# Part B of a decode kernel: keys loaded in whole rows, half of them copied aside by GpSimd, and a softmax in two halves

## The chip, the cores and the metric

The kernel runs on one core of one Trainium2 chip. The time is device microseconds of one execution, as the median of the runs shown. A core has five engines that run beside each other and wait for each other by semaphores: TensorE (PE in the profile), VectorE (DVE), ScalarE (ACT), GpSimd (POOL) and SyncE (SP). Sixteen DMA engines move data between the chip's memory (HBM) and the on-chip memory (SBUF).

## The reference

Two attention steps for one new token (decode) with a cache, side by side. Part A has 32 query heads on 8 key heads and looks at the last W = 2048 positions; part B has 32 query heads with a key head each and looks at all 8192.

```python
def _B_ref(x, k_cache, v_cache, wq, wo):     # x 4x1x512, caches 4x32x8192x128, bf16
    q = (x @ wq).reshape(B, Sq, H, Dh).transpose(0, 2, 1, 3)
    scores = einsum("bhqd,bhkd->bhqk", q, k_cache) * (Dh ** -0.5)
    p = softmax(scores, axis=-1)
    o = einsum("bhqk,bhkd->bhqd", p, v_cache)
    return o.transpose(0, 2, 1, 3).reshape(B, Sq, H * Dh) @ wo
# _A_ref: the same on k_cache[:, :, Sk - W:], v_cache[:, :, Sk - W:] of 8 heads, each repeated 4 times
return concatenate([a, b], axis=-1)
```

Part B's two caches are 2 x 268 MB of the 587 MB that the kernel reads.

## The kernel before, in words

All instructions are first written into one list for each engine (`sch.add`, with what each waits for, and `sch.add_dma` for transfers), and these lists are then issued in order. Where windows between marks repeat (`whole_B`), TensorE, VectorE and ScalarE run them as a loop; SyncE and GpSimd run straight-line code. So the order on an engine is the order in which the Python code adds its instructions, and an instruction that waits holds up everything behind it on its engine.

The work comes in chunks: 8 of part A (numbers 0 to 7), then 32 of part B (8 to 39, `NCA` = 8, `NC` = 40). A chunk of part B is four heads of one batch entry: 256 tiles of 128x128 keys and as many of values, 64 KB in each of 128 partitions, 8.39 MB each. The SBUF tensor `kv` has ten slots of 16 KB per partition: part B's keys lie in slots 0 to 3, its values in 4 to 7, and slots 8 and 9, keys of part A, hold `wol` in part B.

For one chunk (`whole_B`, line 802), with eight tiles to a group and 32 groups:

- `emit_T` transposes eight key tiles on TensorE into one of three PSUM banks `tr`; VectorE (two of three groups, L491) or ScalarE (every third, L489) copies the bank to one of four buffers `kt`. Two groups later (`SLAG`) `emit_S` multiplies it with the query `qq` into the scores `sc`, which have two banks, one for each half of the chunk.
- `stats_rowmax` takes the maxima of each half on VectorE (L560). After the last scores, `stats_gmax` and `stats_bc` make one maximum per head over all rows and its negative `negb` (a transpose and a broadcast on TensorE, two small VectorE steps), and `exp_B` writes the probabilities `pbb` on ScalarE in eight instructions (L606). TensorE meanwhile reorders four blocks of rows of the output weight `wos` (`reorder`), which VectorE copies to `wol` (`take_wol`, L722), and runs fillers (`keep_busy`).
- `emit_pv` multiplies 256 value tiles with the probabilities into the bank `po`; `norm_sum` sums the probabilities over partitions and inverts the sum; `norm_out` writes the weighted output `oz`. The output projection of a chunk (`emit_fin`) runs in the next chunk, after its second group of transposes, and adds up in the PSUM bank `fin` to the end.

The transfers are issued on SyncE in the order wos (every fourth chunk), keys, values (`dma_B`, line 365). Keys come in two halves of 32 KB rows, and the two halves of the buffer come free after the 16th and the 32nd group's transposes. Values come in one transfer of 64 KB rows that waits for the previous chunk's last value product; the last chunks, and the second chunk's values, come in smaller pieces. GpSimd waits for each landing and passes it on to TensorE as a count of groups (`relay`, semaphores `r_k` and `r_v`), so that TensorE's loop can wait on one count. The last two pieces of part A's output weight are loaded at the very end.

## Time and profile before

| | before |
|---|---|
| median of 3 runs | 1370.96 us (1370.92 to 1371.13) |
| the profiled execution, its own time | 1370.91 us |
| its span, first to last instruction | 1369.2 us |
| mean granted TensorE clock | 0.981 |
| VectorE, ScalarE, GpSimd busy | 744.0, 514.2, 9.8 us |
| key and value transfers of part B | 69 and 42 |

The profile is of one execution. A group row reads: line, engine, operation, output <- inputs, shapes, count | busy us, mean ns of one | idle time of the engine ahead of them and what ended it. A timeline row reads: start, length, engine, line, operation and how many of them in a row [idle time before, what ended it]. A row of the chain of waits reads: start, length, what the end was waiting for; the start of a DMA row is its issue and its end the landing. A DMA line counts packets (one to a partition row, and small ones that report the end) and their bytes.

### The profile page before, as it was taken

What the parts mean: (1) busy time and instruction counts of PE and PEld (TensorE: products, weight loads), DVE (VectorE), ACT (ScalarE), POOL (GpSimd) and SP (SyncE); (2) the same over time, 40 slices, a digit from 0 to 9 for tenths busy, and PEclk for the clock granted to TensorE, in tenths of its full rate; (3) what the DMA queues carried; (4) which work ended last, traced back from release to release, by engine and by line L of the source; (5) the groups of instructions that cost most, each with busy time, mean ns of one, the idle gap of its engine ahead of it and who ended that gap; (6) DMA issues with size and microseconds to landing.
All of it is one profiled execution on the core that took longest, in us unless ns stands there. A gap on an engine that the chain in (4) does not pass through costs nothing.

```text
span 1369.2 us, 61524 instructions
## 1 busy us (share of the span) xinstructions
PE 1246.1 (91%) x27801; PEld 1111.7 (81%) x27801; DVE 744.0 (54%) x1335; ACT 514.2 (38%) x649; POOL 9.8 (1%) x29
## 2 busy tenths in 40 slices
...
DMA  9999999999999999999999999999999999999998
GB/s 398 425 428 438 423 432 435 429 434 438 431 431 438 422 433 435 433 439 429 433 433 426 430 437 432 433 438 429 433 431 429 433 436 433 436 433 428 424 426 362
DMA packets 20948, 587.52 MB, mean 429 GB/s; under 512 B 2344, under 2 KB 2368, under 8 KB 4416
## 3 DMA queue, kind: packets, MB, share of 16 engines
...
q8 instruction: 15, 0.25, 0.1%
...
q10 hardware_dynamic: 32, 0.01, 0.0%
HBM read 587.21 MB, written 0.01 MB: 429 GB/s over the span
## 4 chain that ended last, share of the span: by engine, by line
DMA 59%; PE 37%; DVE 2%; issue 1%; ACT 1%; SPq 0%; POOLq 0%; ACTq 0%; DVEq 0%
DMA kv<-in_B_k_cache_dram 36%; PE tr L424 18%; DMA kv<-in_B_v_cache_dram 16%; PE po L426 9%; PE sc L426 8%; DMA wor<-in_A_wo_dram 3%; DMA kv<-in_A_k_cache_dram 2%; DMA kv<-in_B_wq_dram 2%; PE fin L426 1%; PE tr L426 1%; PE ms L426 1%; ACT pba L628 0%; DVE kt L491 0%; DVE sA L544 0%; DVE kv L722 0%
## 5 line engine op out<-in xcount | busy, mean ns | idle before, releaser
L424 PE MATMUL tr<-identb,kv 128*128 128x128 bf16 x8704 | 667.6, 221 | 48.4 <-POOLq L74 40.7
L491 DVE COPY kt<-tr 128x1024 bf16<-128x1024 bf16 x736 | 502.0, 691 | 261.3 <-PE tr L424 258.5
L489 ACT ACTIVATE kt<-tr 128x1024 bf16<-128x1024 bf16 x352 | 359.7, 1024 | 700.8 <-PE tr L424 700.7
L424 PEld LDWEIGHTS tr<-identb,kv 128*128 128x128 bf16 x8704 | 510.0, 99 | 61.0 <-DVE qq L500 42.5
L426 PE MATMUL sc<-qq,kt 128*128 128x64 bf16 x8192 | 399.1, 192 | 12.6 <-DVE kt L491 9.8
L426 PEld LDWEIGHTS sc<-qq,kt 128*128 128x128 bf16 x8192 | 332.8, 98 | 16.1 <-DVE kt L491 13.1
L426 PEld LDWEIGHTS po<-pbb,kv 128*128 128x128 bf16 x8192 | 252.5, 99 | 35.7 <-issue 21.5
L426 PE MATMUL po<-pbb,kv 128*128 128x64 bf16 x8192 | 255.4, 194 | 22.6 <-POOLq L74 21.1
L606 ACT ACTIVATE pbb<-sc,negb 32x128 bf16<-32x128 f32 x256 | 137.9, 539 | 135.4 <-DVE negb L589 132.2
L426 PE MATMUL po<-sel,identb 128*128 128x512 bf16 x352 | 96.1, 382 | 0.0
L722 DVE CAST kv<-tr 128x512 bf16<-128x512 f32 x128 | 80.0, 684 | 0.0
L611 DVE TENSOR_REDUCE rsb<-pbb 128x4 f32<-128x1024 bf16 x32 | 39.0, 1220 | 65.9 <-ACT pbb L606 65.9
L426 PE MATMUL tr<-wos,back 32*128 32x512 bf16 x512 | 66.9, 377 | 3.2
L674 DVE RECIPROCAL rinv<-ms 128x4 f32<-128x4 f32 (+1 forms) x40 | 7.8, 196 | 105.5 <-PE ms L426 105.5
L426 PEld LDWEIGHTS po<-sel,identb 128*128 128x128 bf16 x352 | 26.5, 97 | 47.0 <-issue 27.1
L560 DVE TENSOR_REDUCE rh<-sc 128x4 f32<-128x512 f32 x64 | 43.9, 686 | 14.3 <-PE sc L426 14.3
L426 PEld LDWEIGHTS tr<-wos,back 32*128 32x128 bf16 x512 | 21.4, 93 | 33.7 <-DVE kv L722 18.9
L696 DVE TENSOR_TENSOR oz<-po,rz 128x16 bf16<-128x16 f32 x32 | 5.6, 175 | 68.1 <-PE po L426 68.1
L426 PE MATMUL sc<-qb,kt 128*128 128x64 bf16 (+3 forms) x512 | 25.8, 195 | 1.0 <-issue 0.6
L575 DVE TENSOR_REDUCE gm<-ms 4x4 f32<-4x128 f32 x40 | 11.1, 278 | 28.2 <-PE ms L424 28.2
L426 PE MATMUL po<-pba,kv 128*128 128x64 bf16 x512 | 21.4, 203 | 4.6 <-ACT pba L628 3.1
L426 PEld LDWEIGHTS po<-pba,kv 128*128 128x128 bf16 x512 | 18.8, 105 | 6.8 <-ACT pba L628 5.0
...
## 6 DMA issues: line engine op xcount, KB each, us to landing
...
```

The costliest lines, as they stand in the source:

```text
L424: sch.add("pe", lambda e: e.transpose(o, l, r), waits, key)
L426: sch.add("pe", lambda e: e.matmul(o, l, r, start=start, stop=stop), waits, key)
L489: sch.add("act", lambda e: e.activation(dst, src, ACTF.Copy), waits=waits, key=("ev", s))
L491: sch.add("dve", lambda e: e.tensor_copy(dst, src), waits=waits, key=("ev", s))
L560: sch.add("dve", lambda e: e.tensor_reduce(out=rh[:, half, :], in_=src, axis=AX.X, op=ALU.max), waits=[("S", ch["s"] + (half + 1) * ch["NG ...
L575: sch.add("dve", lambda e: e.tensor_reduce(out=gm[0:C, m, 0:U], in_=src, axis=AX.X, op=ALU.max), waits=[("trm", c)], key=("gmax", c))
L606: sch.add("act", lambda e, src=src, dst=dst, pp=pp, u=u: e.activation(dst, src, ACTF.Exp, bias=negb[pp, 0, u:u + 1], scale=scale), waits=[ ...
L611: sch.add("dve", lambda e: e.tensor_reduce(out=rst[1][:, :], in_=probs_of(c).rearrange("p j u -> p u j"), axis=AX.X, op=ALU.add), waits=[( ...
L674: sch.add("dve", lambda e: e.reciprocal(out=ri, in_=ms[:, L0:L0 + n]), waits=[("L", c)], key=("rinv", c))
L696: sch.add("dve", lambda e: e.tensor_tensor(out=o, in0=i0, in1=i1, op=ALU.mult), waits=waits, key=("oT", c))
L722: sch.add("dve", lambda e: e.tensor_copy(wol[:, u, :], o), waits=[("reord", c) if u == 3 else ("reord", c, u)] + [("fin", prev(c))], key=( ...
```

## The change

Keys. The second half of a chunk's keys gets its place outside the key buffer: `kspare`, slots 8 and 9. Chunks 10 to 34 load their keys in one transfer of 64 KB rows into slots 0 to 3 (`WHOLE`); GpSimd then copies the second half to `kspare`, 16 copies of one group each, as 128x512 int32, each of which counts `r_c` up by one. TensorE takes tiles from 128 on out of `kspare`, and waits for the copies at groups 16 and 24. The next key transfer waits for the transposes of the first half and for all 16 copies. Chunks 8 and 9 and the last five load the keys in pieces, whose second half goes straight to `kspare`. Values come whole but for chunks 8 and 9 and the last three. The landings are passed on in one list after all issues, with a relay of its own for wos (`r_w`) in each chunk.

Softmax. Each half has its own maximum: that of the first half alone, then the running maximum over both. The first half's maximum and exponentials run during the second half's transposes (groups 18 to 26), the second half's during the first value products. The halves' products go to two banks, `po` and `po2` (the third `tr` bank). The first half's sum and product are scaled by the exponential of the maxima's difference (`weigh_B`, `rest_sums`), and its product is added to the second bank by a TensorE product with the identity (`add_first`).

Order. The output weight is reordered at the head of the chunk, in one go into the three `tr` banks and `po`, followed by three fillers instead of eleven, and copied to `wol`, now a tensor of its own; the first three groups of transposes wait for these copies. The output projection follows its own chunk's values. The query copy moves from VectorE to ScalarE. Part A's output weight has two buffers instead of three. The diff, cut:

```diff
+I32 = mybir.dt.int32
-NWO = 3
+NWO = 2
+KMAIN = 128
+WHOLE = (256,)
+HALVES = (128, 128)
+QUARTERS = (64, 64, 64, 64)
 LASTK = (32, 32, 64, 64, 64)
-NEXTK = (64, 64, 64, 64)
-NEXTV = (128, 64, 32, 32)
+NLATE = 5
+NEXTV = (128, 64, 64)
 LASTV = (128, 64, 32, 32)
-SECONDV = (128, 128)
-QK = (0, 4, 8, 16, 24)
-QV = (0, 16, 24, 28)
+QK = (0, 4, 8)
+QC = (16, 24)
+QV = (0, 8, 16, 24, 28)
+NBUSY = 3
...
-        rh = sb("rh", [P, 2, 4], F32)
+        rh = sb("rh", [P, 4], F32)
-        rst = {0: sb("rsa", [P, NSM, 16], F32), 1: sb("rsb", [P, 4], F32)}
+        rsa = sb("rsa", [P, NSM, 16], F32)
+        rsb = sb("rsb", [P, 3, 4], F32)
+        rs2 = sb("rs2", [P, 4], F32)
+        e01 = sb("e01", [P, 4], F32)
+        ib = sb("ib", [P, 2, 4], F32)
+        w1 = sb("w1", [P, 4], F32)
+        t1 = sb("t1", [P, 4], F32)
-        pbt = {0: sb("pba", [P, NPB, NTA * 16 + NW], BF16), 1: sb("pbb", [P, 1, NTB * 4 + NW], BF16)}
+        pbt = {0: sb("pba", [P, NPB, NTA * 16 + NW], BF16), 1: sb("pbb", [P, 2, NTB * 2 + NW], BF16)}
-        wol = kv[:, 8, 0:4 * DO].rearrange("p (u n) -> p u n", u=4)
+        wol = sb("wol", [P, 4, DO], BF16)
+        kspare = kv[:, 8:10, :].rearrange("p s x -> p (s x)")
+        po2 = tr[:, 2, :].bitcast(F32)
...
+                        waits=[("reord", NCA + 4 * hq - 1, 3)] if hq else [], key=("wos", hq))
...
+        def kpieces(c):
+            return QUARTERS if c <= NCA + 1 or c == NC - 2 else LASTK if c == NC - 1 else HALVES if c >= NC - NLATE else WHOLE
+
+        def vpieces(c):
+            return QUARTERS if c == NCA else HALVES if c == NCA + 1 else LASTV if c == NC - 1 else NEXTV if c >= NC - 3 else WHOLE
+
+        def dma_kB(c):
 
             ch = chunks[c]
+            src = B_k[ch["b"], 4 * ch["hq"]:4 * ch["hq"] + 4].rearrange("u (pp j) d -> (u pp) (j d)", pp=P // 4)
+            pieces = kpieces(c)
+            fam = "d_k%d_" % len(pieces)
+            s0 = ch["s"] - ch["NG"]
+            j0 = 0
             for i, n in enumerate(pieces):
-                if part is not None and i != part:
-                    j0 += n
-                    continue
-                waits = []
-                for u in range(j0 // unit, (j0 + n - 1) // unit + 1):
-                    waits += held[at + u]
-                    used[at + u] = [("T", ch["s"] + (u + 1) * unit // TG - 1) if kind == "k" else ("pvh", c) if u < 2 else ("pv", c)]
+                spare = len(pieces) > 1 and j0 >= KMAIN
+                if spare:
+                    dst = kspare[:, (j0 - KMAIN) * P:(j0 - KMAIN + n) * P]
+                    waits = held[8] + held[9] if c == NCA else [("T", s0 + (j0 + n) // TG - 1)]
+                else:
+                    dst = flat(KB, 4)[:, j0 * P:(j0 + n) * P]
+                    if c == NCA:
+                        waits = held[0] + held[1] + held[2] + held[3]
+                    else:
+                        waits = [("T", s0 + min(j0 + n, KMAIN) // TG - 1)]
+                        if j0 + n > KMAIN and len(kpieces(c - 1)) == 1:
+                            waits += [("cp", c - 1)]
                 x = slice(j0 * P, (j0 + n) * P)
-                sch.add_dma("sp", lambda e, x=x: e.dma_start(dst[:, x], src[:, x]), fam + str(i), waits=waits, key=(kind, c, i))
+                sch.add_dma("sp", lambda e, x=x, dst=dst: e.dma_start(dst, src[:, x]), fam + str(i), waits=waits, key=("k", c, i))
                 j0 += n
...
+        def land_kB(c):
+
+            ch = chunks[c]
+            pieces = kpieces(c)
+            s0 = ch["s"] - ch["NG"]
+            j0 = 0
+            for i, n in enumerate(pieces):
+                if len(pieces) == 1:
+                    sch.relay("pool", sems, "r_k", KMAIN // TG, [("k", c, i)])
+                    for g in range(NCP):
+                        x = slice((KMAIN + g * TG) * P, (KMAIN + (g + 1) * TG) * P)
+                        dst, org = kspare[:, g * TG * P:(g + 1) * TG * P].bitcast(I32), flat(KB, 4)[:, x].bitcast(I32)
+                        sch.add("pool", lambda e, dst=dst, org=org: e.tensor_copy(dst, org), waits=[("T", s0 + ch["NG"] - 1)] if g == 0 else [])
+                        emit, waits, _, at = sch.ops["pool"][-1]
+                        sch.ops["pool"][-1] = (emit, waits, ("r_c", 1), at)
+                else:
+                    sch.relay("pool", sems, "r_c" if j0 >= KMAIN else "r_k", n // TG, [("k", c, i)])
+                j0 += n
...
+            sch.tk[("cp", c)] = ("r_c", (n + 1) * NCP)
...
+            pieces = vpieces(c)
+            fam = "d_v%d_" % len(pieces)
+            j0 = 0
+            for i, n in enumerate(pieces):
+                waits = held[4] + held[5] + held[6] + held[7] if c == NCA else [("pv", c - 1, 0 if j0 + n <= NTB // 2 else 1)]
+                x = slice(j0 * P, (j0 + n) * P)
+                sch.add_dma("sp", lambda e, x=x: e.dma_start(dst[:, x], src[:, x]), fam + str(i), waits=waits, key=("v", c, i))
+                j0 += n
...
+            pieces = vpieces(c)
+            for i, m in enumerate(pieces):
+                sch.relay("pool", sems, "r_v", m // TG, [("v", c, i)])
...
+        def land_wos(c):
+
+            sch.relay("pool", sems, "r_w", 1, [("wos", chunks[c]["hq"])])
+            sch.tk[("wr", c)] = ("r_w", c - NCA + 1)
...
-                dma_B("k", c, 0)
                 dma_wos((c - NCA) // NB)
-                dma_B("k", c, 1)
-            else:
-                dma_B("k", c)
-            dma_B("v", c)
+            dma_kB(c)
+            dma_vB(c)
+        for c in range(NCA, NC):
+            land_wos(c)
+            land_kB(c)
+            land_vB(c)
...
+            if kind == "k" and c >= NCA and j >= KMAIN:
+                return kspare[:, (j - KMAIN) * P:(j - KMAIN + 1) * P]
...
-                        waits = [("kr", c, g)] if g in QK else []
+                        waits = ([("kr", c, g)] if g in QK + QC else []) + ([("wol", c, g)] if g < NTRB else [])
...
-                sch.add("dve", lambda e, x=0: e.tensor_copy(qq[:, 0:4], qs[:, bass.ds(x + col, 4)]), at=col,
+                sch.add("act", lambda e, x=0: e.activation(qq[:, 0:4], qs[:, bass.ds(x + col, 4)], ACTF.Copy), at=col,
...
+            dst = rh[:, :] if half else rm[:, 0, :]
+            sch.add("dve", lambda e: e.tensor_reduce(out=dst, in_=src, axis=AX.X, op=ALU.max),
+                sch.add("dve", lambda e: e.tensor_tensor(out=rm[:, 1, :], in0=rm[:, 0, :], in1=rh[:, :], op=ALU.max),
+                        waits=[("rh", c, 1)], key=("rowmax", c, 1))
...
+        def exp_B(c, half, heads):
+            pw = [("c_pb", 1)] + ([("pv", c - 1, half), ("rs", c - 1, half)] if c > NCA else [])
+            for u, pp in [HEADS[u] for u in heads]:
+                src = sc[pp, half, :].rearrange("p (j u) -> p u j", u=4)[:, u, :]
+                dst = probs_of(c, half)[pp, :, u]
+                sch.add("act", lambda e, src=src, dst=dst, pp=pp, u=u: e.activation(dst, src, ACTF.Exp, bias=negb[pp, half, u:u + 1], scale=scale),
+                        waits=[("negb", c, half)] + pw if u == 0 else [], key=("exp", c, half) if u == 3 else None)
+            if 3 in heads:
+                sc_read[half] = [("exp", c, half)]
+
+        def sums_B(c, half):
+            dst = rs2[:, :] if half else rsb[:, 0, :]
+            sch.add("dve", lambda e: e.tensor_reduce(out=dst, in_=probs_of(c, half).rearrange("p j u -> p u j"), axis=AX.X, op=ALU.add),
+                    waits=[("exp", c, half)] + (rs_read[NSM] if half == 0 else []), key=("rs", c, half))
+
+        def weigh_B(c):
+
+            sch.add("dve", lambda e: e.tensor_tensor(out=e01[:, :], in0=negb[:, 1, :], in1=negb[:, 0, :], op=ALU.subtract),
+                    waits=[("negb", c, 1)] + ([("rse", c - 1)] if c > NCA else []), key=("d01", c))
+            sch.add("act", lambda e: e.activation(e01[:, :], e01[:, :], ACTF.Exp), waits=[("d01", c)], key=("e01", c))
...
+                h, jj = j // half, j % half
+                waits = [("exp", c, h)] + (po_read if h == 0 else []) if jj == 0 else []
                 if j == 0:
                     po_read[:] = []
+                waits += [("vr", c, g)] if t == 0 and g in QV else []
+                o = (po2 if h else po)[:, 0:NW]
+                pe_mm(o, tile_of("v", c, j), pbt[1][:, h, jj * 4:jj * 4 + NW], start=jj == 0, stop=jj == half - 1,
+                      waits=waits, key=("pv", c, h) if jj == half - 1 else None)
...
+            pe_mm(ms[:, L0:L0 + 12], onesf[:, :], rsb[:, :, :].rearrange("p x u -> p (x u)"), waits=[("rst", c), "c_onesf"] + ms_read, key=("L", c))
+            lv = ms[:, L0:L0 + 12].rearrange("p (x u) -> p x u", u=4)
+            sch.add("dve", lambda e: e.reciprocal(out=ib[:, :, :], in_=lv[:, 0::2, :]), waits=[("L", c)], key=("rinv", c))
+            sch.add("dve", lambda e: e.tensor_tensor(out=w1[:, :], in0=lv[:, 1, :], in1=ib[:, 0, :], op=ALU.mult), waits=[("rinv", c)], key=("w1", c))
+            sch.add("dve", lambda e: e.tensor_tensor(out=t1[:, :], in0=po[:, 0:4], in1=w1[:, :], op=ALU.mult), waits=[("w1", c), ("pv", c, 0)], key=("t1", c))
...
+        def rest_sums(c):
+
+            sch.add("dve", lambda e: e.tensor_tensor(out=rsb[:, 1, :], in0=rsb[:, 0, :], in1=e01[:, :], op=ALU.mult),
+                    waits=[("rs", c, 0), ("e01", c)], key=("rse", c))
+            sch.add("dve", lambda e: e.tensor_tensor(out=rsb[:, 2, :], in0=rsb[:, 1, :], in1=rs2[:, :], op=ALU.add),
+                    waits=[("rse", c), ("rs", c, 1)], key=("rst", c))
+
+        def add_first(c):
+
+            pe_mm(po2[:, 0:4], identf[:, :], t1[:, :], start=False, stop=False, waits=[("t1", c)], key=("add", c))
+            po_read[:] = [("t1", c)]
...
+                o, i0 = oz[:, :].rearrange("p (b u) -> p b u", b=NB), bcast(po2[:, 0:4], [[0, NB], [1, 4]])
...
+        def reorder(c):
+
+            for u in range(4):
+                pp = slice(u * P // 4, (u + 1) * P // 4)
+                for r in range(4):
+                    pe_mm(reord_at(u), back[pp, r, :], wos[pp, r, :], start=r == 0, stop=r == 3,
+                          waits=[("wr", c), ("c_back", 3)] if u == r == 0 else [],
+                          key=("reord", c, u) if r == 3 else None)
+            po_read[:] = [("wol", c, 3)]
+
+        def take_wol(c):
+            for u in range(4):
+                o = reord_at(u)
+                sch.add("dve", lambda e, u=u, o=o: e.tensor_copy(wol[:, u, :], o), waits=[("reord", c, u)], key=("wol", c, u))
...
-                pe_mm(po[:, :], identb[:, :], sel4[:, :, :].rearrange("p r x -> p (r x)"))
+                pe_mm(sc[:, 1, :], identb[:, :], sel4[:, :, :].rearrange("p r x -> p (r x)"))
...
         def whole_B(c):
 
 
-            ch, p = chunks[c], prev(c)
+            ch = chunks[c]
             sch.mark()
+            reorder(c)
+            keep_busy(NBUSY)
+            take_wol(c)
             emit_qb(c)
             for g in range(ch["NG"]):
                 emit_T(ch["s"] + g)
-                if g == 1:
-                    emit_fin(p)
                 if g >= SLAG:
                     emit_S(ch["s"] + g - SLAG)
-                if g == ch["NG"] // 2 + SLAG + 1:
+                if g == 18:
                     stats_rowmax(c, 0)
+                if g == 20:
+                    stats_gmax(c, 0)
+                if g == 22:
+                    stats_bc(c, 0)
+                if g == 23:
+                    exp_B(c, 0, (0, 1))
+                if g == 26:
+                    exp_B(c, 0, (2, 3))
             for g in range(SLAG):
                 emit_S(ch["s_last"] + 1 - SLAG + g)
             stats_rowmax(c, 1)
-            reorder(c, 0, 0)
-            reorder(c, 1, 1)
-            reorder(c, 2, 2)
-            keep_busy(2)
-            stats_gmax(c)
-            keep_busy(1)
-            stats_bc(c)
-            exp_B(c)
-            for u in range(3):
-                take_wol(c, u, u)
-            keep_busy(3)
-            reorder(c, 3, 0)
-            keep_busy(5)
-            take_wol(c, 3, 0)
-            sums_B(c)
             for g in range(ch["NG"]):
                 emit_pv(c, g)
-                if g == 20:
+                if g == 4:
+                    stats_gmax(c, 1)
+                if g == 8:
+                    stats_bc(c, 1)
+                    sums_B(c, 0)
+                    exp_B(c, 1, (0, 1, 2, 3))
+                    weigh_B(c)
+                    sums_B(c, 1)
+                    rest_sums(c)
+                if g == 24:
                     norm_sum(c)
+                if g == ch["NG"] - 2:
+                    add_first(c)
             norm_out(c)
+            emit_fin(c)
...
-        emit_fin(NC - 1)
+        emit_out(NC - 1)
         emit_fin(NCA - 1)
+        emit_out(NCA - 1)
```

163 lines of the change are left out of this document (69 added, 94 removed).

## Prediction

> **What bounds the kernel now.** I read the page first: its busy line, its DMA lines and the head of the chain.
>
> ```profile
> span 1369.2 us, 61524 instructions
> PE 1246.1 (91%) x27801; PEld 1111.7 (81%) x27801; DVE 744.0 (54%) x1335; ACT 514.2 (38%) x649; POOL 9.8 (1%) x29
> DMA  9999999999999999999999999999999999999998
> HBM read 587.21 MB, written 0.01 MB: 429 GB/s over the span
> DMA 59%; PE 37%; DVE 2%; issue 1%; ACT 1%; SPq 0%; POOLq 0%; ACTq 0%; DVEq 0%
> ```
>
> TensorE and the DMA engines are both over 90%, and the chain names both, so the page alone doesn't say which of them sets the end. The chain in order of time does (start, length, what):
>
> ```profile
> 1.97 27.32 DMA kv<-in_B_wq_dram
> 237.95 30.01 DMA kv<-in_B_v_cache_dram
> 641.70 27.58 DMA kv<-in_B_k_cache_dram
> 680.48 27.59 DMA kv<-in_B_k_cache_dram
> 719.26 27.61 DMA kv<-in_B_k_cache_dram
> 1228.86 27.26 DMA kv<-in_B_k_cache_dram
> 1330.23 36.00 DMA wor<-in_A_wo_dram
> ```
>
> Start plus length is a landing. The key landings at 669.28, 708.07 and 746.87 lie 38.79 and 38.80 us apart. What moves in one of these rounds, the DMA view of that window says; a second window runs from the landing at 1256.12 to the last one, at 1366.23.
>
> ```profile
> DMA packets 432, 16.78 MB, mean 433 GB/s; under 512 B 48, under 2 KB 48, under 8 KB 48
> DMA packets 3419, 45.98 MB, mean 418 GB/s; under 512 B 384, under 2 KB 384, under 8 KB 640
> ```
>
> In a steady round 432 packets carry 16.78 MB: 2 x 128 rows of 32 KB for the keys, 128 rows of 64 KB for the values, and 3 x 16 small ones, 16 to each transfer. The engines hold 433 GB/s with no hole. So TensorE's waits are waits for data, and the end is set by bytes, by what each transfer costs beside its bytes, and by whether the queue is ever empty.
>
> How long the queue is fed ahead, the timeline of one round says:
>
> ```profile
> 630.68 1.06 PE L424 MATMUL tr<-identb,kv 128*128 128x128 bf16 x16 [1.85 <-POOLq L74]
> 653.28 0.35 PE L426 MATMUL sc<-qq,kt 128*128 128x32 bf16 x8 [0.31 <-DVE kt L491]
> 653.57 1.06 PE L426 MATMUL tr<-wos,back 32*128 32x512 bf16 x12
> 656.26 4.42 ACT L606 ACTIVATE pbb<-sc,negb 32x128 bf16<-32x128 f32 x8 [4.06 <-DVE negb L589]
> 657.84 1.25 PE L426 MATMUL po<-sel,identb 128*128 128x512 bf16 x5
> 659.76 5.06 PE L426 MATMUL po<-pbb,kv 128*128 128x64 bf16 x168 [0.66 <-POOLq L74]
> 664.66 0.36 PE L426 MATMUL ms<-rsb,onesf 128*128 128x4 f32 x2
> 664.88 2.73 PE L426 MATMUL po<-pbb,kv 128*128 128x64 bf16 x88
> 667.64 0.33 SPq L386 DMA_DIRECT2D kv<-in_B_v_cache_dram  x1
> 669.46 1.06 PE L424 MATMUL tr<-identb,kv 128*128 128x128 bf16 x16 [1.85 <-POOLq L74]
> ```
>
> Values are asked for at 667.64, when the previous ones have been used. Their transfer starts when the second key half has landed, a quarter round (9.7 us) after 669.28, at 679.0: 11 us ahead. TensorE runs from 630.68 to 667.61 and then has nothing until 669.46.
>
> **The change, part by part.** *Fewer transfers.* From 1256.12 to 1366.23 the program moves half of chunk 37's keys, its values, all of chunks 38 and 39, and two 0.524 MB pieces of wo: 4.19 + 5 x 8.39 + 1.05 = 47.19 MB in 24 transfers (the view counts packets by their start, hence its 45.98). At the steady pace of 38.79 us for 16.78 MB and 3 transfers this is 109.1 us and 8.4 transfers; it took 110.1 us. So 15.6 transfers more cost 1.0 us, 0.065 us each, a size that covers its 128 row packets and 16 small ones together. Part B has 111 key and value transfers now (69 + 42). With the change chunks 10 to 34 have one key transfer each (25), chunks 8 and 9 four each, 35 to 37 two, 38 four, 39 five: 48. Values: 4 + 2 + 27 + 3 + 3 + 4 = 43. 20 transfers fewer are 20 x 0.065 = **-1.3 us**. The reading error of the landings (some 0.3 us in 1.0) bounds this at -0.9 and -1.7 us.
>
> *Copies on GpSimd.* 16 of 128x512 int32 a chunk for 25 chunks. The trace has no such copy; the nearest rows are
>
> ```profile
> L310 POOL TENSOR_SCALAR_AFFINE_SELECT back<-back 128x512 bf16<-128x512 bf16 x4 | 2.5, 637 | 0.6
> L294 POOL MEMSET pm<- 128x512 f32 x1 | 0.5, 525 | 0.0
> ```
>
> With as many elements, one writes and the other reads and writes; I take 0.64 us (0.53 to 1.0), 10.2 us a chunk. Keys land whole at t. The next keys' transfer starts at t + 19.4 (half a round), behind the values. Its issue on SP waits for all 16 copies (t + 10.4) and for the transposes of the first half, half of the 22.95 us from 630.68 to 653.63, so t + 11.5. Then issue 0.33 us and the way to the first byte, which is at most 1.6 us, since the last issue below ends at 1367.63 and all has landed by 1369.2:
>
> ```profile
> 1366.46 1.17 SPq L754 DMA_DIRECT2D out_dram<-outsb  x2
> ```
>
> That makes t + 13.4, 6 us ahead. The cover is gone when a copy takes over (19.4 - 0.2 - 1.9) / 16 = **1.08 us**; from there every 0.1 us costs 1.6 us a chunk. Behind the waiting key transfer on SP stands only the same chunk's value transfer, which isn't due yet. Behind the copies on GpSimd stand the value relay, not due before t + 19.4, and the wos relay behind it.
>
> *Softmax in halves, a running maximum.* The whole-chunk wait goes: between 653.28 and 659.76 TensorE ran reorders and fillers. New TensorE round, from these rows and
>
> ```profile
> L426 PE MATMUL fin<-kv,oz 128*4 128x256 bf16 x264 | 21.9, 293 | 0.0
> L426 PE MATMUL ms<-gm,ind 4*128 4x4 f32 x64 | 12.2, 258 | 5.0 <-DVE gm L575 5.0
> L424 PE MATMUL ms<-identf,rm 128*4 128x128 f32 x40 | 10.9, 272 | 2.7 <-DVE rm L556 2.7
> L606 ACT ACTIVATE pbb<-sc,negb 32x128 bf16<-32x128 f32 x256 | 137.9, 539 | 135.4 <-DVE negb L589 132.2
> L489 ACT ACTIVATE kt<-tr 128x1024 bf16<-128x1024 bf16 x352 | 359.7, 1024 | 700.8 <-PE tr L424 700.7
> L491 DVE COPY kt<-tr 128x1024 bf16<-128x1024 bf16 x736 | 502.0, 691 | 261.3 <-PE tr L424 258.5
> L722 DVE CAST kv<-tr 128x512 bf16<-128x512 f32 x128 | 80.0, 684 | 0.0
> ```
>
> transposes and scores 22.95 - 0.5 (the output projection leaves this stretch) = 22.4; two maximum transposes (0.27) and broadcasts (two passes of 0.26), 2 x 0.8 = 1.6; values 7.8 with the sum; waiting for the second half's four exponentials 4 x 0.54 = 2.2 us, of which eight groups of values (2 us) hide all but about 0.5; add_first, two passes like the broadcast, 0.5; output projection 8 x 21.9 / 264 = 0.7 and some 0.4 until DVE has made oz; 16 reorders 1.06 to 2.1, taken as 1.4; three fillers at 1.25 / 5 = 0.75. Together 36.1 us, against 38.8: 2.7 us spare. The values' issue comes at t + 0.2 + 22.4 + 1.6 + 7.8 + 1.0 = t + 33.0, with the 1.9 us t + 34.9, against t + 38.8: 4 us ahead instead of 11. What is late next would be this one. A chunk's extra work on the others is small: DVE gets some eight instructions of 0.17 us and the four reorder casts (4 x 0.68 = 2.7 us) move to the head of the chunk; ACT gets the query copy (0.17) and one exponential. In the transposes' stretch ACT has one eviction of 1.02 us in every three groups (3 x 22.95 / 32 = 2.15 us), so the first half's 2.2 us fit between. All this I cost at nothing; without the 2.7 us of cover it would cost its excess once a round, 25 times.
>
> *TensorE's clock.* Idle TensorE has its price here, as two stretches of the window view show (us, busy time of each engine, granted clock, DMA share, GB/s), the first a steady round, the second a slow stretch:
>
> ```profile
> 669.29:708.07 38.78, 35.70 (x808) 31.72 (x808) 21.24 (x36) 14.55 (x18) 0.00 (x0) 1.00 1.00 433
> 514.20:517.60 3.40, 3.40 (x41) 2.89 (x38) 1.08 (x3) 1.02 (x1) 0.00 (x0) 0.51 1.03 443
> ```
>
> 3.4 us at 0.51 lose 1.7 us of work. Two in one round would use up the 2.7 us; one leaves 1.0, and less idle makes the next slow stretch less likely. The Trainium skill (TensorE: Matmul & The Clock Gate, Part 1, What's actually happening) says that half rate follows an idle window of about 3.4 us. By that rule a round that keeps TensorE waiting under 3 us would rarely be throttled; the row agrees on the length, though its idle before was only about 1.85 us.
>
> *Instructions.* GpSimd gets 400 copies and some 12 relays more, straight-line code that comes over the same DMA engines. The DMA view from the second projection weight's landing (29.29) to the values at 267.96:
>
> ```profile
> q1 hardware_dynamic: 5016, 102.47, 100.2%
> q8 instruction: 13, 0.21, 0.4%
> ```
>
> By the code, that stretch moves 102.2 MB in 35 transfers. At the steady pace it is 236.4 us with 18.3 transfers; 16.7 more add 1.1 us; it took 238.67. So 1.2 us go to 13 loads of 16 KB, 0.09 us each on average. The page counts 15 such loads for the whole program's code:
>
> ```profile
> q8 instruction: 15, 0.25, 0.1%
> ```
>
> For 400 instructions more I allow three, 3 x 0.09 = 0.3; if each hit the engine that is last, at 16 KB by 433 / 16 GB/s, 0.6 us each, it is 1.8; if other code shrinks by as much, nothing. I take **+0.3**.
>
> *Entry and tail.* The entry's keys and values in quarters are in the count of transfers; the second key half there waits for part A's last transposes, which the queue of 20 us covers. At the tail the last landing is a piece of wo, and part B's output is ready before it. Nothing, within 0.3 us either way.
>
> *Sum:* -1.3 + 0.3 = -1.0, so the profiled execution's 1370.91 (its span 1369.2 and 1.7 around it; 0.05 under the median of 1370.96) becomes **1369.9 us**. The bounds give 1368.9 to 1372.1.
>
> **The rivals.** *A. GpSimd and DVE shut each other out (slower).* If a copy holds SBUF against DVE's eviction and the other way round, a copy takes 0.64 + 0.69 = 1.33 us in turn with L491, 16 take 21.3 us, and the next keys' first byte comes at t + 23.4 instead of t + 19.4: 4 us late, 25 times, 1470 us. For it: both work through the whole first half of a round. Against it: nothing in the trace, where GpSimd is idle after 12 us. The Trainium skill (SBUF — State Buffer, Who interferes with whom) calls the shared port pair an exclusive lock, but only for DVE in a two-port mode or with two SBUF inputs, and L491 reads PSUM. By that rule this rival doesn't happen for the evictions; no run here shows it yet. Chance 0.06.
>
> *B. TensorE's round becomes the bound (slower).* It decides when the round passes 38.8, or the values' issue t + 36.9. If stalls in the new interleaving and one slow stretch in each round add 5 us, the round is 41.1: 2.3 us x 25 = 58 us, 1428; just past the edge (0.3 us a round) it is 1377. For it: lead falls from 11 to 4 us, and 1.7 us of slow clock are possible. Against: 2.7 us spare. Chance 0.14.
>
> *C. A whole transfer saves more than the tail shows (faster).* Where transfer and load costs both come out at their best, twice the 0.065 (2.6 us) and no lag from loads at the entry (1.2 us), it is 1367.1. For it: two unknowns of the same sign. Against: the 1.0 us of the tail leaves no room for twice. Chance 0.13.
>
> *D. The transfers don't get cheaper* (their number costs nothing, the tail's 1.0 us is something else): 1371.2, no change. It is within my own case's range.
>
> **How the numbers follow.** A change under 0.2% (2.74 us) can't be told from none here. My case, D with it, has 0.67 and lies within that; C 0.13; A and B together 0.20. So faster 0.13, same 0.67, slower 0.20. My case alone is 1368.9 to 1372.1. For eight in ten the range goes down to C's 1367.0 and up to the nearer part of B, 1377.
>
> **What would show it.** Right: key landings in the chain 38.7 us apart in the middle of part B, 433 GB/s in each slice, GpSimd copies near 0.64 us, SP's issue of keys near t + 12 and of values near t + 33. Rival A would show as copies over 1.08 us or L491 over 0.69 us; B as holes in the DMA line with TensorE full; C as rounds under 38.6 us. I'd be wrong if the DMA share of any 100 us in the middle drops below 0.99.

## The result and the profile after

| | before | after |
|---|---|---|
| median | 1370.96 us (19 runs, 1370.61 to 1373.06) | 1376.78 us (19 runs, 1372.43 to 1379.53) |
| profiled execution, its span | 1370.91, 1369.2 us | 1376.78, 1375.0 us |
| granted TensorE clock | 0.981 | 0.963 |

After over before is 1.0036, with a 95% interval of 1.0027 to 1.0046 (taken over all the runs; the two medians alone give 1.0042): slower, by 0.4%. The prediction said 1369.9 us. The time lies in its range (1367.0 to 1377.0), on the other side of no change than was forecast.

The page after, with the lines that answer to those of before:

```profile
span 1375.0 us, 62434 instructions
PE 1200.1 (87%) x27697; PEld 1123.1 (82%) x27697; DVE 770.3 (56%) x1559; ACT 520.7 (38%) x713; POOL 234.5 (17%) x429
DMA  9999999999999999999999999999999999999997
q8 instruction: 21, 0.34, 0.1%
q14 instruction: 8, 0.07, 0.0%
HBM read 587.21 MB, written 0.01 MB: 427 GB/s over the span
L564 DVE COPY kt<-tr 128x1024 bf16<-128x1024 bf16 x736 | 503.2, 691 | 290.1 <-PE tr L493 287.1
L421 POOL COPY kv<-kv 128x512 int32<-128x512 int32 x400 | 224.6, 616 | 923.1 <-DMA kv<-in_B_k_cache_dram 923.1
```

The same bytes, the DMA line full but for its last slice, GpSimd's copies as quick as taken (616 ns), VectorE's eviction not slowed (691 ns before and after). Loads of instructions stand in two rows: q8 has 21 of 16 KB where the page before has 15, and q14 has 8 of 8 KB where it has 5. Otherwise almost nothing has happened on this page, and yet 5.8 us of span were lost. Nor do windows of 100 us in the middle of part B show it (us, busy time of each engine, clock, DMA share, GB/s):

```profile
620.00:720.00 100.00, 89.04 (x2084) 82.81 (x2081) 55.84 (x112) 37.37 (x54) 19.92 (x36) 0.97 1.00 430
720.00:820.00 100.00, 90.84 (x2107) 86.44 (x2105) 58.91 (x111) 41.42 (x54) 25.00 (x45) 0.97 1.00 431
820.00:920.00 100.00, 84.99 (x1942) 79.07 (x1939) 51.91 (x107) 33.01 (x47) 22.37 (x40) 0.93 0.99 429
```

Holes of one microsecond don't show in such views; the landings show them. In the chain of waits a key transfer's start plus its length is its landing:

```profile
571.71 29.29 DMA kv<-in_B_k_cache_dram
...
613.98 25.73 DMA kv<-in_B_k_cache_dram
650.40 28.78 DMA kv<-in_B_k_cache_dram
...
885.70 29.76 DMA kv<-in_B_k_cache_dram
928.23 25.93 DMA kv<-in_B_k_cache_dram
964.85 28.99 DMA kv<-in_B_k_cache_dram
```

601.00, 639.71, 679.18: a round of 38.71 us, shorter than before (38.80), then one of 39.47. 915.46, 954.16, 993.84: 38.70 and 39.68. The landing events of all transfers say which one is late: always the values. From the trace, with the lead (landing of the keys ahead less the values' issue) and the hole (how much later the values land than 19.35 us, half a round of 38.7 us, after the keys):

```
values' issue   keys ahead landed   lead   hole
635.92          639.71              3.79   0.79
672.33          679.18              6.84   0.00
714.25          717.89              3.64   0.00
792.86          796.57              3.71   1.03
871.33          875.00              3.67   0.48
950.18          954.16              3.98   1.00
1065.29         1072.64             7.35   0.00
```

Eight such holes, of 0.08 to 1.03 us, make 4.1 us; six of them have leads of 3.65 to 4.06 us, and the two with long leads (7.05 and 8.02) are of 0.12 and 0.19 us. Long and short leads alternate. The timeline of TensorE in two rounds that follow each other says why:

```profile
595.49 0.82 PE L495 MATMUL sc<-sel,identb 128*128 128x512 bf16 x3
601.17 2.74 PE L493 MATMUL tr<-identb,kv 128*128 128x128 bf16 x24 [4.86 <-POOLq L80]
...
637.75 0.82 PE L495 MATMUL sc<-sel,identb 128*128 128x512 bf16 x3
639.88 1.51 PE L493 MATMUL tr<-identb,kv 128*128 128x128 bf16 x24 [1.30 <-POOLq L80]
...
674.17 0.82 PE L495 MATMUL sc<-sel,identb 128*128 128x512 bf16 x3
679.35 2.74 PE L493 MATMUL tr<-identb,kv 128*128 128x128 bf16 x24 [4.36 <-POOLq L80]
```

After the fillers TensorE has nothing until the keys land: 4.86 us, then 1.30, then 4.36. After the long waits the first 24 transposes take 2.74 instead of 1.51 us. The window view puts the clock beside it:

```profile
599.50:606.30 6.80, 5.13 (x57) 5.14 (x58) 2.07 (x3) 1.02 (x1) 5.15 (x10) 0.50 0.98 424
639.70:646.50 6.80, 6.62 (x147) 6.49 (x148) 4.79 (x8) 2.90 (x3) 6.64 (x12) 1.00 1.03 445
678.00:684.80 6.80, 5.45 (x63) 5.46 (x64) 2.19 (x4) 1.02 (x1) 5.47 (x10) 0.50 0.96 414
```

Half clock for 6.8 us, from 521 us on in every second round: the slow round makes TensorE late, so it waits less ahead of the next one, which runs at full clock, is early, and waits long again. The values' issue follows the keys' landing by 32.6 us in a full-clock round (672.33 - 639.71) and by 35.1 in a slow one (714.25 - 679.18).

The rest of the loss is at the tail. The DMA view of the last 40 us counts there (loads, MB, share):

```profile
q8 instruction: 6, 0.10, 1.0%
```

And TensorE's timeline in that stretch, the rows in which it waited for its own instructions, and the first of the output projection:

```profile
1348.68 0.34 PE L495 MATMUL sc<-qq,kt 128*128 128x64 bf16 x6 [1.19 <-issue]
1355.43 0.22 PE L493 MATMUL tr<-identb,kv 128*128 128x128 bf16 x1 [0.74 <-issue]
1361.90 0.19 PE L495 MATMUL po<-pbb,kv 128*128 128x64 bf16 x1 [1.24 <-issue]
1368.11 1.22 PE L495 MATMUL tr<-pbb,kv 128*128 128x64 bf16 x36 [0.94 <-issue]
1371.67 0.28 PE L495 MATMUL fin<-wol,oz 128*4 128x256 bf16 x2 [0.27 <-DVE oz L800]
```

The six loads of 16 KB that the page has more than before all lie here, at 1339.5, 1346.2, 1353.0, 1359.4, 1365.6 and 1369.2 us, and each of the four stalls of 0.7 to 1.2 us with nothing to wait for ("issue") begins 1.3 to 1.7 us behind the start of one: 4.1 us of TensorE. Beside that, the first two value pieces of the last chunk land 10.93 and 5.16 us after the piece ahead, against 9.71 and 4.90 before: 1.5 us. Part B's output (`oz`) is made at 1371.44, after the last landing (1370.02); before, it was there at 1365.06, 1.2 us ahead of the last landing (1366.23), and the end came 3.0 us behind that landing. Now it comes 5.0 behind. The two rows, before and after:

```profile
1365.06 0.17 DVE L696 TENSOR_TENSOR oz<-po,rz 128x16 bf16<-128x16 f32 x1 [2.07 <-PE po L426]
1371.44 0.18 DVE L800 TENSOR_TENSOR oz<-tr,rz 128x16 bf16<-128x16 f32 x1 [1.12 <-PE tr L495]
```

The sum: the keys of the last chunk land 2.3 us later than before (holes of 4.1 where before had none, and some -1.8 from cheaper transfers), its values lose 1.5, the end 2.0 more: 5.8 us, the two spans' difference.

### The profile page after: what moved, and what is told of

Its sections match the earlier page's. It is cut to its first block, busy times and chain, and to the rows that moved or that the text cites. A ratio compares the mean times of both kernels' runs of the same rounds, so it can differ in the third digit from the quotient of the medians.

```text
span 1375.0 us, 62434 instructions
## 1 busy us (share of the span) xinstructions
PE 1200.1 (87%) x27697; PEld 1123.1 (82%) x27697; DVE 770.3 (56%) x1559; ACT 520.7 (38%) x713; POOL 234.5 (17%) x429
## 4 chain that ended last, share of the span: by engine, by line
DMA 48%; PE 44%; issue 3%; DVE 3%; ACT 2%; ACTq 0%; SPq 0%; DVEq 0%; POOLq 0%
DMA kv<-in_B_k_cache_dram 43%; PE tr L493 24%; PE sc L495 11%; PE tr L495 4%; PE po L495 3%; DMA kv<-in_B_v_cache_dram 2%; DMA kv<-in_B_wq_dram 2%; PE ms L495 1%; DMA kv<-in_A_k_cache_dram 1%; DVE kt L564 1%; DVE wol L833 1%; ACT pba L716 1%; ACT pbb L686 1%; PE fin L495 1%; DVE sA L617 0%
## 5 line engine op out<-in xcount | busy, mean ns | idle before, releaser
L421 POOL COPY kv<-kv 128x512 int32<-128x512 int32 x400 | 224.6, 616 | 923.1 <-DMA kv<-in_B_k_cache_dram 923.1
L495 PE MATMUL tr<-pbb,kv 128*128 128x64 bf16 x4096 | 135.6, 193 | 27.4 <-ACT pbb L686 25.5
L495 PEld LDWEIGHTS tr<-pbb,kv 128*128 128x128 bf16 x4096 | 130.9, 99 | 31.2 <-issue 30.3
L495 PE MATMUL po<-pbb,kv 128*128 128x64 bf16 x4096 | 135.1, 194 | 5.5 <-issue 4.4
L495 PEld LDWEIGHTS po<-pbb,kv 128*128 128x128 bf16 x4096 | 127.5, 98 | 5.3 <-issue 3.3
L833 DVE CAST wol<-tr 128x512 bf16<-128x512 f32 x96 | 60.4, 685 | 54.3 <-PE tr L495 52.6
L693 DVE TENSOR_REDUCE rs<-pbb 128x4 f32<-128x512 bf16 x32 | 22.0, 686 | 50.3 <-ACT pbb L686 50.3
L495 PE MATMUL tr<-wos,back 32*128 32x512 bf16 x384 | 34.8, 383 | 0.4 <-issue 0.4
L495 PE MATMUL po<-wos,back 32*128 32x512 bf16 x128 | 33.9, 384 | 0.0
L495 PE MATMUL sc<-sel,identb 128*128 128x512 bf16 x96 | 26.9, 390 | 0.0
## 6 DMA issues: line engine op xcount, KB each, us to landing
kv<-in_A_k_cache_dram SPq DMA_DIRECT2D x8, 2048.0 KB, 14.1
```

Of the source, the lines that this page charges most:

```text
L421: sch.add("pool", lambda e, dst=dst, org=org: e.tensor_copy(dst, org), waits=[("T", s0 + ch["NG"] - 1)] if g == 0 else [])
L495: sch.add("pe", lambda e: e.matmul(o, l, r, start=start, stop=stop), waits, key)
L693: sch.add("dve", lambda e: e.tensor_reduce(out=dst, in_=probs_of(c, half).rearrange("p j u -> p u j"), axis=AX.X, op=ALU.add), waits=[("ex ...
L833: sch.add("dve", lambda e, u=u, o=o: e.tensor_copy(wol[:, u, :], o), waits=[("reord", c, u)], key=("wol", c, u))
```

## The experiments

Two causes were in question. **Late values**: half clock makes the values' issue late, and their transfer leaves holes. **The last chunk's code**: in the changed kernel `emit_fin` stands inside `whole_B`, and its last product closes the accumulation for the last chunk alone (`stop=... and c == lastc`, L850). So chunk 39's window differs from the 31 ahead of it, it isn't part of TensorE's loop, and it runs as straight-line code that has to be loaded. The kernel before was timed again beside each set of runs: 1370.86, 1371.17, 1370.84 and 1370.94 us median. One table ahead (stretches, holes, landings and ends are those of the profiled execution; fillers are those of one chunk, 0.226 us each; half-clock stretches are counted over the whole record, which in every run but e5_loop_fillers has one at its very end, and then from 250 to 1240 us alone):

| run | fillers | half-clock stretches: all, 250 to 1240 us | holes at values, us | last landing | end behind it | median (lowest to highest), us | ratio (95%) |
|---|---|---|---|---|---|---|---|
| before | 11 | 13, 9 | 0 | 1366.23 | 3.0 | 1370.96 | 1 |
| after | 3 | 18, 13 | 4.1 | 1370.02 | 5.0 | 1376.78 (1372.43 to 1379.53) | 1.0036 (1.0027 to 1.0046) |
| e1_loop | 3 | 19, 13 | 6.8 | 1371.73 | 3.0 | 1370.69 (1369.65 to 1376.67) | 1.0007 (0.9995 to 1.0018) |
| e2_fillers | 18 | 4, 0 | 0 | 1365.86 | 8.5 | 1376.18 (1376.17 to 1376.41) | 1.0038 (1.0025 to 1.0051) |
| e3_vhalves | 3 | 16, 11 | 0 | 1367.86 | 3.7 | 1373.24 (1372.65 to 1374.91) | 1.0016 (1.0007 to 1.0025) |
| e4_khalves | 3 | 18, 12 | 0.1 | 1367.97 | 6.4 | 1375.74 (1375.36 to 1376.24) | 1.0034 (1.0021 to 1.0047) |
| e5_loop_fillers | 18 | 2, 0 | 0 | 1364.49 | 9.7 | 1376.02 (1375.93 to 1376.25) | 1.0035 (1.0021 to 1.0048) |
| e6_loop_vhalves | 3 | 18, 13 | 0 | 1366.88 | 3.0 | 1371.59 (1371.37 to 1371.98) | 1.0002 (0.9992 to 1.0011) |
| e7_loop_mid_fillers | 12 | 10, 3 | 0.6 | 1364.99 | 5.9 | 1372.85 (1371.36 to 1374.04) | 1.0008 (0.9999 to 1.0018) |
| e11_loop_7 | 7 | 16, 10 | 0.3 | 1364.65 | 3.8 | 1371.90 (1370.18 to 1374.23) | 1.0004 (0.9995 to 1.0013) |
| e12_loop_0 | 0 | 27, 20 | 4.2 | 1369.05 | 3.0 | 1374.03 (1370.06 to 1378.96) | 1.0014 (1.0001 to 1.0027) |

**The last chunk back in the loop.** The closing flag is taken from chunk 39, and two products with zeros close the accumulation behind the loop.

```diff
-                          stop=i == len(ops) - 1 and c == lastc, waits=...
+                          stop=i == len(ops) - 1 and c == NCA - 1, waits=...
...
+        for h, (p0, x) in enumerate(out_halves(1)):
+            pe_mm(fin[p0:p0 + NB, 0:DO // 2], qb[:, 0, 32:32 + NB], wol[:, 0, x], start=False, stop=True, key="close" if h else None)
```

> One part of the change undone: the last chunk's output projection no longer closes the accumulation itself (two products with zeros after the loop do), so that TensorE's loop covers chunk 39 again. Theory: six instruction loads of 16 KB at the end vanish; they cost 1.5 us of landings (10.93 and 5.16 instead of 9.71 and 4.89 us) and 2.0 us between the last landing and the end (5.0 instead of 3.0). Median 1376.8 - 3.5 = 1373.3 us, spread as before. Rival, the longer chain at the tail (second half's maximum, add_first, sums) makes the end late: only the 1.5 us go, 1375.3 us, and the last landing still lies 5 us ahead of the end.

The median fell by 6.1 us, more than expected, for chance has a part in it: seven of the twelve runs took 1369.65 to 1371.08 us, the others up to 1376.67. The profiled one (1376.50) has 6.8 us of holes, but no instruction load in its tail, no stall for "issue", and an end 3.0 us behind the last landing. The tail of that run:

```profile
1365.55 2.27 PE L495 MATMUL tr<-pbb,kv 128*128 128x64 bf16 x72 [0.83 <-ACT pbb L686]
1369.42 0.87 PE L495 MATMUL tr<-pbb,kv 128*128 128x64 bf16 x24 [0.68 <-POOLq L80]
1371.01 0.60 PE L495 MATMUL fin<-wol,oz 128*4 128x256 bf16 x8 [0.27 <-DVE oz L800]
```

TensorE now waits for data here (its wait at 1369.42 is for the landed values), not for its own code. The difference of the two ratios, 0.0029, is 4.0 us, beside 3.5 from the tail's sum. That the loads are what delays the landings, all the runs of the table bear out: the four with loads of 16 KB in the tail (after, e2, e3, e4) have there one piece that lands 0.9 to 1.4 us late, and the seven without any have none over 0.1 us.

**Fillers, to take the idle time away.** `NBUSY = 18` in the changed kernel, so 15 x 0.226 = 3.4 us more work while TensorE waits.

> One number changed: 18 fillers at the head of a chunk instead of 3, 15 x 0.25 = 3.7 us of TensorE work in its wait for the keys. Theory: the value transfer is asked for late in every second round because TensorE, idle for some 5 us, falls to half clock for 6.8 us; without that idle time the clock stays at full rate, the values are asked for 6 us ahead in every round, and the holes of 4.1 us in the landings vanish: 1376.8 - 4.1 = 1372.7 us, and the runs spread by under 1 us. Rival, values are late since the transposes start only when the whole keys have landed, whatever the clock: as the changed kernel, 1376.8 us, or later since the fillers stand in the way.

In the middle the theory came out: no half-clock stretch from 250 to 1240 us, no hole, the last landing 4.2 us earlier than after, and runs within 0.24 us of each other. The time didn't fall, since the end now comes 8.5 us behind the last landing. The fillers run in the last chunks too, where TensorE has no idle time to fill.

**Values in halves**, whose first half is asked for when the first half's products are done:

```diff
-            return ... NEXTV if c >= NC - 3 else WHOLE
+            return ... NEXTV if c >= NC - 3 else HALVES
```

> One part changed: values in two transfers of 32 KB rows in every chunk, the first of which waits only for the first half's product. Theory (a value transfer needs some 4.5 us from its issue to its first bytes, and has 3.7 to 4 us in slow rounds): the first half is asked for some 4 us earlier, the holes vanish at the same clock, and 27 more transfers cost 27 x 0.065 = 1.8 us: 1376.8 - 4.1 + 1.8 = 1374.5 us. Rival, the holes come from something else than the late issue (instruction loads, GpSimd): 1376.8 + 1.8 = 1378.6 us.

No hole, though the clock is nearly as slow as after (16 stretches); the median is 1.3 us under what was expected. So it is the issue's lateness that makes the holes, and the clock that makes it late. This run also halves the rows; but whole rows leave no hole over 0.2 us either where the changed kernel asks for them 4.8 us ahead or more.

**Keys in halves, no copies** (`kpieces` returns `HALVES` from chunk 10 on; GpSimd copies nothing):

> One part undone: keys in two transfers of 32 KB rows in every chunk from 10 on, second half straight to its place, no GpSimd copies; softmax in halves as in the change. Theory: 25 more transfers cost 25 x 0.065 = 1.6 us, the first half's landing lets the transposes start 9.7 us earlier, so TensorE idles elsewhere and the values are asked for further ahead; holes vanish: 1376.8 - 4.1 + 1.6 = 1374.3 us. Rival, GpSimd's copies hold up VectorE: evictions shorter than 691 ns, and the gain is larger than 2.5 us.

VectorE's eviction without any copy beside it, in this run:

```profile
L564 DVE COPY kt<-tr 128x1024 bf16<-128x1024 bf16 x736 | 501.6, 690 | 209.2 <-PE tr L493 206.5
```

690 ns against 691: the copies don't hold VectorE up. The time was 1.4 us over what was expected: the landings lost the holes, but the end came 6.4 us behind the last one, with the last chunk's code still straight-line.

**Both cures together.** e5_loop_fillers is e1_loop with 18 fillers, e6_loop_vhalves e1_loop with values in halves, e7_loop_mid_fillers e1_loop with 12 fillers.

> Last chunk in the loop as in e1_loop, and 18 fillers a chunk as in e2_fillers. My theory has two separate costs: values asked for late behind a half clock (some 4.1 us in the changed kernel), and a last chunk outside TensorE's loop (1.5 us of landings and some 2 us behind the last landing). Both gone, the last landing comes 1.5 us before that of e2_fillers (1365.9), at 1364.4, with no instruction load after 1300 us; the time has no spread over 0.5 us. The fillers fill TensorE's round (33 to the values' issue, 1.5 of projection and reorders, 4.06 of fillers: 38.6 of 38.7), so the last two chunks come late by up to 2 x 3.4 us less what the tail has to spare; I expect the end 5 us behind the last landing and 1371 us in all. Rival: the 8.5 us of e2_fillers behind the last landing were the code loads alone; then the end is 3 us behind the last landing and the time 1369.1.

> Last chunk in the loop as in e1_loop, and all values in two halves, whose first half is asked for when the first half of the products is done. By my theory no hole is left behind the keys though the half-clock windows stay (15 to 19), last landing 1366.4 (1367.9 in e3_vhalves less 1.5 for the code loads), end 3 us later, 1371.1 in all, with no spread over 1 us; the 27 transfers more cost 27 x 0.065 = 1.8 us against the runs of e1_loop without holes (1369.7). Rival, that the values' issue had nothing to do with the holes: spread from 1370 to 1377 as in e1_loop, plus 1.8.

> Last chunk in the loop, 12 fillers a chunk instead of 3. They take 2.7 us instead of 0.7 out of TensorE's idle time of some 4.9 us, which leaves about 2.9 and 1.3 us of slack for the tail. By my theory fewer half-clock windows (5 to 13 instead of 19), so few or no holes over 0.3 us; last landing 1364.6 to 1366, end 3 to 3.5 us later, 1369.7 in all, 0.1% under the kernel before. Rival, that half clock needs no more than 2 us of idle time: windows and holes as in e1_loop, 1370 to 1376.

The landings came as expected in all three (1364.49, 1366.88, 1364.99). e6 is right to half a microsecond, and its runs lie within 0.6 us: hardly any spread is left once the values are asked for in time. Against e11_loop_7 (1364.65 with a hole of 0.25) its 27 transfers more cost 2.5 us, 0.09 each. e5 and e7 were wrong at the tail, and so in time by 5.0 and 3.2 us: the ends came 9.7 and 5.9 us behind the last landing, with no instruction load there, so the rival of e5 is wrong too. The one hole of e7 (0.57 us) is no late issue: its lead was 6.06 us, and it lies beside a load of 8 KB (below). In e5's steady round the reason can be read:

```profile
669.30:708.00 38.70, 37.08 (x830) 33.17 (x827) 22.04 (x43) 14.75 (x20) 8.98 (x16) 1.00 1.00 434
```

37.1 of 38.7 us are work. The tail's pieces are there for TensorE to catch up, and it can't any more. 12 and 18 fillers put the end 2.9 and 6.7 us later than 3: about twice 0.226 a filler (chunks 38 and 39), less at most 1.1 us of slack. That rule was put to the test with 7 and with no fillers:

> Last chunk in the loop, 7 fillers a chunk. With 0.226 us each they take 0.9 us more of TensorE's idle time than 3 fillers, and leave about 4. At the tail the 12 and 18 fillers put the end 2.9 and 6.7 us later, which is 2 x 0.226 a filler less 1.1 us of slack; 4 more fillers give 1.8 - 1.1 = 0.7: end 3.7 us behind the last landing. Half-clock windows between those of e7_loop_mid_fillers (10) and e1_loop (19), say 15; fewer holes over 0.3 us than in the changed kernel, lasting 1 to 2 us in all instead of 4. Time 1370.4, range 1369.9 to 1373. It beats the kernel before only if the holes stay under 1 us in all.

> Last chunk in the loop and no fillers: the other end of the same row. TensorE idles 0.7 us longer a round, so by my theory at least as many half-clock windows as e1_loop (19 or more) and holes at the values of 4 to 8 us, spread of several us; the end stays 3 us behind the last landing, since there the store is what ends it. Time 1370 to 1377, median 1373. Rival, that the fillers themselves cost time in the middle of part B (TensorE's round): 0.5 to 1 us less than e1_loop, with fewer holes.

The ends came as the rule has it, 3.8 and 3.0 us behind the last landing, and the stretches too: 16 and 27. e12's median (1374.03) and holes (4.2 us) are as expected. e11's median (1371.90) is above the 1370.4 expected, though its profiled run is at 1370.18 with one hole of 0.25 us, beside a load of 8 KB; its other runs go up to 1374.23, for a reason that no trace shows. From 18 fillers to none the stretches go 2, 10, 16, 19, 27, and the spread of the runs with them: 0.3, 2.7, 4.0, 7.0 and 8.9 us.

**Leads set on purpose.** e5_loop_fillers, with hardly a half-clock stretch, and the values' issue held back behind later work:

```diff
+                if len(pieces) == 1:
+                    waits += [[], [("reord", c, 3)], [("wol", c, 0)], [("wol", c, 2)]][c % 4]
```

> e5_loop_fillers with the values of three of four chunks asked for later on purpose, at full clock: one in four as it was (lead before the landing of the keys ahead 6.1 us), one after the reorders (lead 4.1), one after the first copy of the weight (3.4), one after the third (2.3). My theory says that the first byte of a values' transfer needs some 4.6 us behind its issue: holes of 0, 0.5, 1.2 and 2.3 us, with 6, 7 and 7 chunks of the last three some 27 us in all, so 1398 us. Rival (the prediction's 1.9 us to the first byte; the holes of the changed kernel then come from the clock or something else): no hole in any, the time of e5_loop_fillers.

1391.75 us (2 runs; ratio 1.0149, 1.0130 to 1.0167), 15.7 over e5_loop_fillers, with 16.3 us of holes in the profiled run (1393.99) and only four half-clock stretches from 250 to 1240 us: lateness makes them, without the slow clock. But not at the rate expected (27 us). Leads of 7.4 us and more had holes of 0.2 at most; of 19 leads between 1.97 and 4.61 us, five had none, the others 0.1 to 2.2 us, and at one lead (2.7 to 2.9 us) both 0.0 and 2.2 occur. The packets of two such transfers, from the trace, in us behind the values' issue:

```
                                      issue 681.30, lead 2.65, hole 0.00    issue 364.34, lead 2.73, hole 1.91
keys' last rows end on 16 engines     1.40 to 2.31                          1.54 to 2.37
values' first rows start              1.41 to 2.32                          1.75 to 3.29
they take                             2.42 to 2.89                          2.42 to 3.44
```

The first row starts 1.4 to 1.8 us behind the issue here, and 0.95 us behind it where engines were idle by then (issue of 642.51 in this run): the prediction's 1.9 us hold for the first engine. But they don't hold for all sixteen. On the right one row starts only 3.29 us behind the issue, though the keys' last row had ended at 2.37, and rows that start in the first 3.5 us behind an issue take up to 1.0 us longer than the usual 2.42 (in the changed kernel, at the issue of 792.86, one took 4.20). Nor do the engines run dry at the landing: the first of them is done 1.2 us ahead of it here, and 2.0 us at 792.86.

Which of these late rows leaves a hole can be read from the trace. An engine that starts late or slowly costs nothing as long as its first row of values ends within one usual row (2.42 us) of the last of the keys' rows; what the latest first row ends beyond that is the hole (us behind the issue):

```
run, issue          lead   keys' last row ends, + 2.42   latest first row ends   beyond   hole
after 714.25        3.64   5.65                          5.65                    0.00     0.00
after 792.86        3.71   5.74                          6.77                    1.03     1.03
after 950.18        3.98   5.94                          7.08                    1.13     1.00
e8_leads 681.30     2.65   4.73                          4.73                    0.00     0.00
e8_leads 364.34     2.73   4.80                          6.73                    1.93     1.91
```

In the traces of the kernels before and after and of the runs with whole values, 67 values' transfers (those that land from 200 to 1215 us) have a lead under 4.75 us; for 64 of them this gives the hole to 0.25 us, for the others to 0.6. Some 200 have leads of 4.8 us and more, and just four of these have a hole over 0.25 us. The four, at leads of 6.06 to 6.14 us in e7, e9 and e10, lie beside instruction loads: in e7 a load of 8 KB at 994.76 takes one engine 0.31 us and makes the row behind it 0.35 us longer. A like load in e5, at 996.08, left no hole. Why some first rows are late or slow and others, at the same lead, aren't, is not shown.

**Fillers only ahead of the tail.** 18 fillers up to chunk 34 (or 36) and 3 behind, so TensorE's loop becomes two loops:

```diff
-            keep_busy(NBUSY)
+            keep_busy(NBUSY if c < NC - 5 else 3)
```

> As e5_loop_fillers, but 18 fillers only up to chunk 34 and 3 in chunks 35 to 39, which makes TensorE's loop two loops. From the ends behind the last landing (3.0 us with 3 fillers, 5.9 with 12, 9.7 with 18) I read that a filler of 0.226 us counts about twice at the tail, in chunks 38 and 39, where TensorE's round has no slack. Then the end is 3 us behind the last landing again. The second loop's code is loaded once, in chunk 35: some 7 instruction loads near 1160 to 1210 us, up to 1.5 us of landings; last landing 1364.5 to 1366, end 1367.5 to 1369, time 1370.2, no holes at the values, spread under 0.5 us. That would be under the kernel before by some 0.05%. Rival, that the late end has another cause than the fillers of the last chunks: end 8 to 10 us behind the last landing, 1375.

> The same with the switch two chunks later: 18 fillers up to chunk 36, 3 in chunks 37 to 39, so the second loop's code is loaded in chunk 37, where TensorE has less time left to make up the stalls. By my theory of the tail (each us of TensorE lost from chunk 37 on counts in full, as 9.7 us of early key halves and 2.7 us of slack a round are all there is): end 3 to 6 us behind the last landing, last landing as in e9_fillers_to_34, time 1370.5 to 1373. Rival (code loads cost nothing but their share of a DMA engine): equal to e9_fillers_to_34.

Both failed: 1389.84 us (ratio 1.0145, 1.0125 to 1.0166) and 1380.58 (1.0066, 1.0053 to 1.0080). The code of the second loop cost more than the fillers. In e9 the waits of TensorE in the stretch where it is loaded first (engine, line, waited for, total, times, longest):

```profile
PE tr L493 <- issue: 2.7, 1, 2.7
PE tr L495 <- issue: 2.7, 1, 2.7
PE po L495 <- issue: 2.1, 2, 1.8
PE sc L495 <- issue: 1.1, 1, 1.1
```

8.6 us in one chunk, which makes its values late (a hole of 3.49); and near 1338 us the code is loaded once more, with a stall of 6.28 us. These loads begin with the first instructions of the last chunk (its reorders, at 1344.50), so that chunk seems to have fallen out of the second loop; why, stays open. e10 ends 14.1 us behind its last landing, with 8.2 us of such stalls. Stalls of 8.6 and 6.3 us against the 4.1 in the changed kernel's tail: late instructions are a price of their own here, and neither run says anything of the fillers.

No version is clearly under the kernel before. e1_loop comes nearest: six of its twelve runs are 0.6 to 1.2 us under 1370.86, but its ratio isn't under 1.

## Why the prediction was wrong, step by step

**Fewer transfers: right in kind, mis-sized.** Predicted -1.3 us, bounds -0.9 and -1.7. Without late code and holes (e5_loop_fillers) the last landing is at 1364.49 against 1366.23: -1.7. A transfer, taken as 0.065 us from the tail, is 0.09 by this (1.74 / 20) and 0.09 by e6, at the edge of what was allowed.

**Copies on GpSimd: right.** 616 ns against 0.64 us taken, edge 1.08. The keys' issue at 650.40 is t + 10.7 (predicted t + 11.5). Rival A is out: 691 and 690 ns with and without copies.

**Softmax in halves: the round right, the wait behind it mis-sized.** TensorE's values came at t + 32.6 where the clock was full, against t + 33.0. The step that failed is what follows from it: "with the 1.9 us t + 34.9, against t + 38.8: 4 us ahead instead of 11". The 1.9 is an issue of 0.33 us and a way to the first byte of at most 1.6, which had been read at the end of the kernel, from two small stores. A first byte did come that soon, 0.95 us behind the start of an issue at the earliest. The Trainium skill (DMA: Bandwidth & Descriptors, Specifications) gives a first-byte latency of some 0.6 us for this path; counted from the end of the 0.33 us that the issue takes, the 0.95 us agree. What the step left out is that all sixteen engines have to get their first rows, that the last of these comes as late as 3.55 us behind the issue (792.86 in the changed kernel, with the keys' last row done at 3.32), and that some of them are slow. In the changed kernel leads of 3.6 to 4.1 us left holes of up to 1.0 us, in e12_loop_0 4.7 still 0.2, and from 4.8 us on late values left none. With keys that land some 38.7 us apart, that puts the edge near t + 34, not t + 36.9: the reserve at full clock was 1.4 us (34 less 32.6), not 4. The step named the transfer that would be late next, and priced its lateness at nothing.

**TensorE's clock: right in kind, the wrong way round in size.** The step expected that one half-clock stretch would leave 1.0 us and that "less idle makes the next slow stretch less likely". TensorE did less, so it idled more: 3.6 to 5.3 us in one piece ahead of the slow stretches from 521 us on, where the kernel before idled 1.85 to 1.95. Those stretches were 6.8 us in every second round rather than 3.4 us in some; they moved the values by 2.5 us (35.1 against 32.6) where the step had 1.7, and so past the edge. The fillers that the change took out had kept the clock up: 18, 12, 7, 3 and none leave 0, 3, 10, 13 and 20 stretches between 250 and 1240 us. The page of the Trainium skill that the prediction named (TensorE: Matmul & The Clock Gate, Part 1, What's actually happening) has half rate follow an idle window of about 3.4 us: the waits of 4.36 and 4.86 us agree. The prediction's reading of it, rarely under 3 us, does so only in part: e7, whose longest wait in the middle of part B was 2.9 us, still had three stretches there, each of 3.4 us, and the kernel before nine with waits of 1.95 at most (the row that the prediction quotes is one). With waits of at most 1.63 us, in e2 and e5, there was none.

**Instructions: looked for on the wrong engine.** The step counted GpSimd's copies (+0.3) and "if other code shrinks". The three loads that it allowed did come (q14, 8 for 5; the step's own 15 are q8 alone), and one of them costs 0 to 0.65 us where its effect can be seen (near 995 us in e5, e7 and e10). What it missed was TensorE's last chunk. **Entry and tail: "Nothing, within 0.3 us either way"** is the other step that failed: "part B's output is ready before" the last landing was true before and not after, since the projection moved into the chunk with a closing flag for the last one. The runs showed 1.5 us of landings and 2.0 behind them, and e1_loop took both away.

**The rivals.** B had the place and nearly the time: a values' issue just past the edge, 1377. Its condition never came: TensorE still waited 1.30 us at the end of a slow round, and its values were asked for at t + 35.1 at the latest, short of t + 36.9. The edge itself lay 3 us earlier. The sign by which the prediction would be wrong (a DMA share under 0.99 in some 100 us) never came, too coarse to see 4 us in 900. B had 0.14, too little for a step that had cut a lead from 11 to 4 us. C and D are out: rounds without a hole took 38.70 us, and transfers did get cheaper. A gain of the size forecast was there in the fastest runs of e1_loop alone (1369.65).

So: -1.8 for the transfers, +4.1 for late values, +1.5 and +2.0 for the last chunk's code. Shown by runs are the last two (e1_loop), the late values (e3, e6, e8) and the clock behind them (the row of fillers). How one late issue leaves a hole and the next none can be read from the rows; why their first rows differ is not shown.
